# A chunked RWKV attention and token mixer on one Trainium2 core: recurrent state held as diagonal blocks, V of one batch loaded whole, and a new order of steps

## The chip, the cores and the metric

The kernel runs on one core of a Trainium2 chip. The metric is the device time of that core in microseconds, the median of the runs shown. The kernel before takes 106.95 us (three runs, 106.95 to 108.07). Inputs and output are float32 in device memory; the products inside are bf16 with float32 sums.

## The reference

Two layers follow each other. The first is a linear attention with a state of 48 x 48 for each of 4 batches and 8 heads; the second mixes the tokens of a batch:

```python
for t in range(S):                                   # S = 768, heads H = 8, D = 48
    cur = einsum('bhd,bhe->bhde', u * k[t], v[t])
    y[t] = einsum('bhd,bhde->bhe', r[t], state + cur)
    state = w[t][..., None] * state + einsum('bhd,bhe->bhde', k[t], v[t])
x = y.transpose(0, 2, 1, 3).reshape(B, S, H * D)     # 4 x 768 x 384
wq, wk = x @ w_q, x @ w_k                            # 64 wide
mixed = (wq @ wk.T) * scale @ x
out = relu(mixed) @ w_out
```

## The kernel before

**Tiling.** A unit is 256 tokens of one batch (two chunks c = 0, 1 of 128), so there are 12 units, three per batch. Two heads (a pair hp, with hh = 0, 1) share the 128 partitions: head hh lies in partitions 64 hh to 64 hh + 47. Function `unit` adds the steps of one unit to a plan: loads of w, k, r, v (384 KB each); logarithm of w (`f_ln`), cast of k and r (`f_c16`), a triangular product that sums the logarithms (`f_cw`), its exponentials `ep` and `en`; transposes of k and r on TensorE (`f_rawT`), RT = r * ep, KT = k * en, scores A = KT x RT per chunk (`f_A`) and their mask (`f_am`), the state, the output `y`, then X, its transpose, and the q and k of the mixer (`f_qk`). The last unit of a batch also forms T = wk' x X over the six chunks (`f_T`), and from it three blocks of relu, output product and store (`f_mx`, `f_rl`, `f_fp`, `f_os`, `f_st`).

**State.** `f_sn` adds the old state (one product with the identity, 384 columns) and four products of 96 columns, one per head pair. These also give the two blocks that mix the heads of a pair. `f_sb` multiplies by `ptm`, which holds the decay for a head's own columns and zero for the other head's; `ptm` is made on GpSimd (`f_ptm`). So the four products of 96 columns with the old state in `f_y` can take all 128 partitions at once.

**V.** A token pair lies in one partition after the ordinary load (runs of 384 bytes). For V the tokens must be put apart. Units whose digit in `DIRECT` (L339) is 0 (five of them) do so with a cast on GpSimd (`f_v16`), a product with a permutation (`f_vp`) and a copy (`f_vb`). The seven others load V with four DMAs of 96 KB in runs of 192 bytes (`load_v`, L226) and need one cast (L562).

**Order.** Nothing is ordered at run time but by semaphores. Each engine has an in-order queue, and so has SP, which issues the loads and stores. The list `RANK` gives each step its place in its engine's queue, and `ENG` the engine where there is a choice. `Plan.order` walks the queues with assumed durations, to assign PSUM banks and to emit the instructions. Tiles of loads rotate over four buffers, most others over two. `warm` adds products with a zero tile Z: 26 after the first unit's steps and 16 at the end, beside nine before the first step.

**Set-up.** L245 to L293 fill constants and clear padded tiles on DVE, ahead of everything else in its queue; the first useful step there is the cast of k (L475).

Of the kernel before, what the change touches and what calls it, by code (L numbers as in the profile page):

```python
# [14 lines left out]
AX = mybir.AxisListType  # L15
# [9 lines left out]

class Plan:

    def __init__(self, kinds, switch):
        self.kinds = kinds
        self.switch = switch
        self.steps = []

    def add(self, eng, dur, rank, fn, after=(), fill=None, read=(), lag=100, mode=0,
            behind=None):
        s = dict(mode=mode, behind=behind, eng=eng, dur=dur, rank=rank, fn=fn, after=[a for a in after if a is not None],  # L40
                 fill=fill, lag=lag, n=len(self.steps), out=[])
        s["buf"] = None if fill is None else dict(readers=[])
        self.steps.append(s)
        for a in read:
            self.reads(s, a)
        return s

    def dma(self, issue, dur, rank, fn, after=(), fill=None, read=()):

        i = self.add("SP", issue, rank, fn, after, fill, read, lag=0)  # L50
        m = self.add("DQ", dur, 0, self.nothing, [i], lag=0)
        return i, self.add(f"L{m['n']}", 1950, 0, self.nothing, [m], lag=0)

    def nothing(self):
        pass

    def reads(self, s, a, own=False):

        if not own:
            s["after"].append(a)  # L60
        if a["buf"] is not None:
            a["buf"]["readers"].append(s)

    def order(self):
        never = 1 << 60
        queues = {e: [] for e in ("PE", "ACT", "DVE", "POOL", "SP")}
        for s in sorted(self.steps, key=lambda s: s["rank"]):
            if s["eng"] in queues:
                queues[s["eng"]].append(s)
            for a in s["after"]:  # L70
                a["out"].append(s)
        free = dict.fromkeys(queues, 0)
        free["DQ"] = 0
        place = dict.fromkeys(queues, 0)
        rings, owners, moved, done, mode = {}, [None] * 8, [], [], 0

        def clear(buf):

            if buf is None:
                return 0  # L80
            return max([x.get("end", never) for x in buf["readers"]], default=0)

        def start(s):

            if any("end" not in a for a in s["after"]):
                return never, None
            if s["behind"] is not None and "start" not in s["behind"]:
                return never, None
            t = max([free[s["eng"]]] + [a["end"] for a in s["after"]])
            if s["behind"] is not None:  # L90
                t = max(t, s["behind"]["start"])
            if s["eng"] == "SP" and len(moved) >= 3:
                t = max(t, moved[-3])
# [13 lines left out]
            if s["fill"] is not None:  # L107

                ring, size = rings.setdefault(s["fill"], []), self.kinds[s["fill"]]
                if len(ring) >= size:  # L110
                    t = max(t, clear(ring[-size]))
# [7 lines left out]
        while True:  # L119
# [7 lines left out]
            if at is not None:  # L127
                s["buf"]["bank"] = at
                for x in range(at[0], sum(at)):
                    owners[x] = s["buf"]  # L130
            elif s["fill"] is not None:
                rings[s["fill"]].append(s["buf"])
            change = e == "PE" and s["mode"] != mode
            if e == "PE":
                mode = s["mode"]
            run(s, t, s["dur"] + self.switch * change)
            if e == "SP":
                for m in s["out"]:
                    if m["eng"] == "DQ":
                        run(m, max(free["DQ"], s["end"]), m["dur"])  # L140
                        moved.append(free["DQ"])
                        for x in m["out"]:
                            if x["eng"].startswith("L"):
                                run(x, m["end"], x["dur"])
        assert len(done) == len(self.steps)
        return done


@with_exitstack
def kernel(  # L150
# [14 lines left out]
    C = 128  # L165
# [9 lines left out]
    HW = H * D2  # L175

    SHIFT = 25
    MU = -SHIFT * math.log(2.0) / C

    def mm(o, l, rr, start=True, stop=True, trans=False):  # L180
        nc.tensor.matmul(o, l, rr, start=start, stop=stop,  # L181
                         skip_group_check=True, is_transpose=trans)
# [4 lines left out]
    sm = ctx.enter_context(tc.tile_pool(name="sm", bufs=3))  # L187
    bt = ctx.enter_context(tc.tile_pool(name="bt", bufs=2))
# [6 lines left out]
    NB = 4  # L195
    WG = [const([C, HW], F32, f"wg{i}") for i in range(NB)]
    RG = [const([C, HW], F32, f"rg{i}") for i in range(NB)]
    KG = [const([C, HW], F32, f"kg{i}") for i in range(NB)]
    VG = [const([C, HW], F32, f"vg{i}") for i in range(NB)]
    NOS = 4  # L200
    OS = [const([C, 2 * DM], F32, f"os{i}") for i in range(NOS)]
    EW = 132

    KDS = [const([C, 1024], BF16, f"kd{i}") for i in range(2)]
    LW = [const([C, 2 * H * 64], BF16, f"lw{i}") for i in range(2)]
    R16 = [const([C, 2 * H * 64], BF16, f"r16{i}") for i in range(2)]
    K16 = [const([C, 2 * H * 64], BF16, f"k16{i}") for i in range(2)]
    QK = [const([C, NU * 384], BF16, f"qk{i}") for i in range(2)]
    TS = [const([C, DM], BF16, f"ts{i}") for i in range(2)]
    EP = [const([C, 8 * EW], BF16, f"ep{i}") for i in range(2)]  # L210
# [9 lines left out]

    def load_v(b, i, tl):

        for c in range(2):
            src = v[b, :, ds(i * U + c * C, C)].rearrange("h (q j) d -> j q h d", j=2)
            for j in range(2):
                nc.sync.dma_start(out=view(tl, c * DM, [[D, H], [1, D]], p0=64 * j, pn=64),  # L226
                                  in_=src[j])
# [6 lines left out]
    ID16 = const([C, C], BF16, "ID16")  # L234
    Z = const([C, 512], BF16, "Z")
    US = const([C, C], F32, "US")
    CM = const([C, 2 * C], BF16, "CM")
    PM = const([C, 2 * C], BF16, "PM")
    MB = const([C, 2], F32, "MB")
    pos0 = const([C, 1], mybir.dt.int32, "pos0")  # L240
    pos1 = const([C, 1], mybir.dt.int32, "pos1")
    gx = const([C, 1], F32, "gx")
    gv = const([C, 1], F32, "gv")

    nc.vector.memset(Z, 0.0)  # L245
    for _ in range(9):
        mm(PS[:, ds(0, 512)], Z[:, ds(0, C)], Z)
    nc.vector.memset(uT, 0.0)  # L248
    for hh in range(2):
        nc.scalar.dma_start(out=view(uT, hh, [[2, NP], [1, 1]], p0=hh * 64, pn=D),  # L250
                            in_=dataclasses.replace(u, offset=hh * D,
                                                    ap=[[1, D], [D2, NP], [1, 1]]))

    nc.vector.memset(CM, 1.0)
    nc.vector.memset(US, 1.0)
    nc.vector.memset(ID16, 0.0)
    nc.vector.memset(PM, 0.0)
    for t in LW:
        nc.vector.memset(t, 0.0)
    for t in TS:  # L260
        nc.vector.memset(t[64:128, :], 0.0)
    for t in EP:
        nc.vector.memset(view(t, 0, [[EW, 8], [1, 1]]), 1.0)
    for t in R16 + K16 + KDS:
        nc.vector.memset(t, 0.0)  # L265
    nc.vector.memset(MB, 0.0)
    nc.vector.memset(MB[0:D, 0:1], 2.0 ** -SHIFT)
    nc.vector.memset(MB[64:64 + D, 1:2], 2.0 ** -SHIFT)

    for j in range(2):  # L270
        nc.gpsimd.iota(pos0[ds(64 * j, 64), :], pattern=[[0, 1]], base=j, channel_multiplier=2)
        nc.gpsimd.iota(pos1[ds(64 * j, 64), :], pattern=[[0, 1]], base=j + 1,
                       channel_multiplier=2)
    nc.scalar.activation(gx, pos0, ACT.Exp, bias=0.0, scale=MU)
    nc.scalar.activation(gv, pos1, ACT.Exp, bias=0.0, scale=-MU)
    for c in range(2):
        for j in range(2):
            m = view(CM, j * C, [[64, 2], [1, 64]], p0=c * 64, pn=64)
            nc.gpsimd.affine_select(m, m, pattern=[[1, 2], [2, 64]], compare_op=ALU.is_ge,
                                    fill=0.0, base=-j, channel_multiplier=-2)  # L280
    for c in range(2):
        for j in range(2):
            m = PM[ds(c * 64, 64), ds(j * C + j * 64, 64)]
            nc.gpsimd.affine_select(m, m, pattern=[[1, 64]], compare_op=ALU.not_equal,
                                    fill=1.0, base=0, channel_multiplier=-1)
    nc.gpsimd.affine_select(ID16, ID16, pattern=[[1, C]], compare_op=ALU.not_equal, fill=1.0,
                            base=0, channel_multiplier=-1)
    for j in range(2):
        m = view(US, 0, [[64, 2], [1, 64]], p0=j * 64, pn=64)
# [627 lines left out]
```

## Time and profile before

| what | value |
|---|---|
| median of three runs | 106.95 us |
| span of the profiled execution, first to last instruction | 105.2 us |
| granted TensorE clock | 1.000 |
| products with the zero tile Z | 51 |
| ACT waiting for a load of w | 5.1 us in 4 waits |
| GpSimd waiting for loads of v, k and r | 4.5 + 2.0 + 1.5 us, and 1.4 us for v in the seven units of `load_v` |
| last ordinary load issued | about 72 us (r), V of the last unit 77 to 80 us |
| DMA issues of V: 384 KB / 96 KB | 5 / 28 |

The span is measured inside the execution. The 1.75 us between it and the median lie before the first and after the last instruction. PE is TensorE, DVE the vector engine, ACT the scalar engine, POOL GpSimd; SPq is SP's queue. All TensorE instructions have line L181 since one helper issues them, so they are told apart by their operands.

### The profile page before, as it was taken

Reading aid. Unit: us, or ns where it says so; the run is one execution under the profiler, and the core shown is the slowest. Engines: PE = TensorE matmul, PEld = TensorE weight load, DVE = VectorE, ACT = ScalarE, POOL = GpSimd, SP = SyncE. Lnnn points to the kernel's source line nnn. Section 1 sums busy time; section 2 is a strip of 40 time slices with the busy share of each in tenths; the row PEclk is TensorE's granted clock in tenths of the full one; section 3 lists DMA queues with packets and bytes.
Section 4 is the critical chain, followed back from the end, with each engine's and each line's share of the span. In section 5 each row is a group of like instructions: output and inputs, shape, how many; then the busy total and the mean of one; then the engine's idle time right before and its main releaser. Section 6 shows DMA issues by size and latency. Waiting matters only on the chain.

```text
span 105.2 us, 3714 instructions
## 1 busy us (share of the span) xinstructions
PE 96.2 (91%) x1506; PEld 70.2 (67%) x1506; DVE 88.1 (84%) x138; ACT 79.9 (76%) x123; POOL 71.0 (67%) x92
## 2 busy tenths in 40 slices
PE   5969889997999998999997897779999999998995
PEld 2246566686887786968796775658697987856551
DVE  6898997898999999798999996786998889754740
ACT  4367778797989868997899959867898895954610
POOL 6600859599997996979979993968689699000000
DMA  1999999999999898989997969998997870033564
GB/s 28 298 324 325 325 323 270 238 297 175 312 316 264 148 272 230 288 172 310 325 311 142 213 123 269 350 289 209 288 255 143 303 307 18 0 153 150 199 243 160
DMA packets 61217, 24.62 MB, mean 234 GB/s; under 512 B 58896, under 2 KB 60048, under 8 KB 61200
## 3 DMA queue, kind: packets, MB, share of 16 engines
q1 hardware_dynamic: 60640, 24.19, 85.5%
q10 hardware_dynamic: 560, 0.20, 0.7%
q8 instruction: 11, 0.18, 0.7%
q14 instruction: 6, 0.05, 0.1%
HBM read 19.66 MB, written 4.72 MB: 232 GB/s over the span
## 4 chain that ended last, share of the span: by engine, by line
PE 51%; DVE 14%; DMA 13%; issue 7%; POOL 5%; ACT 4%; SPq 4%; DVEq 0%; ACTq 0%; POOLq 0%
PE PS L181 51%; DMA wg<-in_w_dram 7%; DMA kg<-in_k_dram 6%; SPq L226 3%; DVE SB L666 2%; DVE RT L536 2%; POOL KT L547 2%; DVE qT L529 2%; DVE KT L547 2%; POOL Vd L601 1%; ACT MX L381 1%; SPq L230 1%; ACT kd L373 1%; DVE X L707 1%; DVE kd L265 1%
## 5 line engine op out<-in xcount | busy, mean ns | idle before, releaser
L619 DVE TENSOR_TENSOR AM<-PS,US 128x1024 bf16<-128x1024 f32 x24 | 28.9, 1220 | 1.1 <-PE PS L181 0.7
L547 POOL TENSOR_TENSOR KT<-ks,en 128x1024 bf16<-128x1024 bf16 (+1 forms) x10 | 19.3, 1934 | 1.2 <-ACT en L498 0.6
L601 POOL TENSOR_TENSOR Vd<-VB,dd 128x768 bf16<-128x768 bf16 (+1 forms) x14 | 18.4, 1318 | 2.2 <-ACT dd L371 1.3
L181 PE MATMUL PS<-Z 128*128 128x512 bf16 x51 | 16.2, 424 | 1.5 <-DVE uT L248 1.2
L707 DVE SCALAR_TENSOR_TENSOR X<-PS,gx,Vd 128x768 bf16<-128x768 f32 (+1 forms) x13 | 12.3, 955 | 3.3 <-PE PS L181 2.8
L181 PEld LDWEIGHTS <-KT 48*128 48x128 bf16 (+1 forms) x272 | 10.7, 95 | 6.3 <-issue 3.8
L467 ACT ACTIVATE lw<-wg 128x768 bf16<-128x768 f32 x12 | 10.0, 846 | 5.5 <-DMA wg<-in_w_dram 5.1
L181 PE MATMUL PS<-wo,MX 128*128 128x384 bf16 x72 | 13.5, 326 | 0.1
L504 ACT ACTIVATE ep<-PS 128x1024 bf16<-128x1024 f32 (+1 forms) x14 | 12.7, 922 | 0.9 <-PE PS L181 0.9
L498 ACT ACTIVATE en<-PS 128x1024 bf16<-128x1024 f32 (+1 forms) x14 | 12.5, 904 | 0.5 <-issue 0.3
L666 DVE TENSOR_TENSOR SB<-PS,ptm 128x384 bf16<-128x384 f32 x20 | 11.1, 553 | 1.5 <-PE PS L181 1.3
L181 PE MATMUL PS<-RT,KT 48*128 48x128 bf16 x192 | 9.2, 217 | 1.4 <-POOL KT L547 0.5
L381 ACT ACTIVATE MX<-PS 128x768 bf16<-128x768 f32 (+1 forms) x12 | 8.7, 730 | 1.8 <-PE PS L181 1.7
L475 POOL CAST r<-rg 128x768 bf16<-128x768 f32 x10 | 8.7, 870 | 1.6 <-DMA rg<-in_r_dram 1.5
L475 POOL CAST k<-kg 128x768 bf16<-128x768 f32 x9 | 7.4, 825 | 3.3 <-DMA kg<-in_k_dram 2.0
L181 PE MATMUL PS<-ID,k 128*128 128x128 bf16 x96 | 7.4, 220 | 2.2 <-POOL k L475 1.4
L181 PEld LDWEIGHTS <-MX 128*128 128x128 bf16 x72 | 6.7, 98 | 3.9 <-issue 0.3
L373 ACT ACTIVATE kd<-PS,gv 128x384 bf16<-128x384 bf16 (+1 forms) x11 | 8.1, 740 | 1.4 <-PE PS L181 1.3
L181 PEld LDWEIGHTS <-Z 128*128 128x128 bf16 x51 | 5.0, 105 | 6.0 <-issue 2.3
L371 ACT COPY os<-PS 128x768 f32<-128x768 f32 (+1 forms) x10 | 7.1, 708 | 2.5 <-PE PS L181 2.2
L536 DVE TENSOR_TENSOR RT<-PS,ep 128x1024 bf16<-128x1024 bf16 (+1 forms) x14 | 8.4, 609 | 0.5 <-PE PS L181 0.2
L181 PE MATMUL PS<-CM,lw 64*128 64x128 bf16 x192 | 7.8, 223 | 1.1 <-ACT XT L371 0.7
(82 smaller groups left out, 211.4 us busy)
## 6 DMA issues: line engine op xcount, KB each, us to landing
wg<-in_w_dram SPq DMA_DIRECT2D x12, 384.0 KB, 5.3
kg<-in_k_dram SPq DMA_DIRECT2D x12, 384.0 KB, 5.0
rg<-in_r_dram SPq DMA_DIRECT2D x12, 384.0 KB, 5.1
out_dram<-os SPq DMA_DIRECT2D x9, 384.0 KB, 4.3
vg<-in_v_dram SPq DMA_DIRECT2D x28, 96.0 KB, 3.7
vg<-in_v_dram SPq DMA_DIRECT2D x5, 384.0 KB, 5.0
out_dram<-os SPq DMA_DIRECT2D x5, 192.0 KB, 2.0
wof<-in_moe_w_out_dram SPq DMA_DIRECT2D x1, 576.0 KB, 5.7
```

Source lines behind the costliest of these rows:

```text
L181: nc.tensor.matmul(o, l, rr, start=start, stop=stop, skip_group_check=True, is_transpose=trans)
L381: nc.scalar.activation(o, i, ACT.Relu)
L467: nc.scalar.activation(view(lw, 0, [[64, H], [512, 2], [1, D]]), view(wg, 0, [[D2, H], [D, 2], [1, D]]), ACT.Ln, bias=0.0, scale=math.exp( ...
L475: op(view(dst, 0, [[64, H], [512, 2], [1, D]]), view(src, 0, [[D2, H], [D, 2], [1, D]]))
L498: nc.scalar.activation(sb("en", [C, 1024])[:, cols(cs, 512)], t["cw"][:, cols(cs, 512)], ACT.Exp, bias=0.0, scale=-1.0)
L504: nc.scalar.activation(view(ep, cs[0] * NP * EW + 66, [[EW, NP * len(cs)], [-65, 2], [1, 64]]), t["cw"][:, cols(cs, 512)], ACT.Exp, bias=0 ...
L536: nc.vector.tensor_tensor(view(sb("RT", [C, 1024]), cs[0] * 512, [[C, n4], [64, 2], [1, 64]]), view(t["rT"], cs[0] * 512, [[C, n4], [64, 2 ...
L547: e.tensor_tensor(sb("KT", [C, 1024])[:, cols(cs, 512)], t["ks"][:, cols(cs, 512)], t["en"][:, cols(cs, 512)], ALU.mult)
L601: nc.gpsimd.tensor_tensor(sb("Vd", [C, 2 * DM])[:, cols(cs, DM)], t["VB"][:, cols(cs, DM)], view(t["dd"], cs[0] * H, [[1, len(cs) * H], [0 ...
L619: nc.vector.tensor_tensor(view(sb(f"AM{c}", [C, 1024]), 0, [[C, 8], [1, C]]), view(t[f"A{c}"], 0, [[C, 8], [1, C]]), view(US, 0, [[0, 8], ...
L666: nc.vector.tensor_tensor(view(x, 0, [[D, H], [1, D]]), view(t[f"sn{c}"], 0, [[D, H], [1, D]]), view(t["ptm"], c * 8, [[1, 8], [0, D]]), A ...
L707: nc.vector.scalar_tensor_tensor(view(X["t"], (2 * i + c0) * DM, [[DM, ncs], [1, DM]]), view(t["y"], c0 * 512, [[512, ncs], [1, DM]]), gx, ...
```

## The change

The step planner and `unit` are written anew; the arithmetic that is kept has the same instructions. What differs:

- **State.** The state tile has 192 columns: head hh of pair hp in partitions 64 hh on, columns 48 hp on. `kd` is stored with zeros around each head, so that a window of 128 columns puts a head's result into the right partitions; eight products of 48 columns take the place of four of 96. The decay is read from `ep`; `ptm` and its constant are gone. The factor that was in `ptm` moves into `kd` and the identity.
- **Output.** The state's part of y becomes products over 48 partitions (`yi`), four for each chunk and head half, issued ahead of the scores' part (`ya`). A second half that goes to the same chunk is preceded by a drain of TensorE. 
- **T.** The two chunks of a unit go to two halves of the array's columns and of the output partitions.
- **V.** `DIRECT` is gone. Nine units use the ordinary load, permutation and copy. The last batch's V (three units) is loaded by four DMAs of 288 KB in runs of 192 bytes, in two steps of the plan.
- **Set-up.** Only the padding is cleared, and only part of it before the second tiles' turn; the permutation's constant is made later on POOL.
- **Fillers.** 12 products with Z, all ranked within the first two units' steps; none at the end. The nine before the first step stay.
- **Order.** New `RANK` and `ALT` (engine choices), planned with 1190 ns for a load in the first three units and 1440 after, where 1440 stood for all (1780 for the first).

The instructions' order on PE has 92 changes between whole-array products and those on part of it (cw, vp, A, yi, T), against 56 in the trace of before. SP issues, after the loads of units 0 to 3: `vw` (V of the last batch) behind k of unit 11, then the first store, then w and r of unit 11.

```diff
-    mm(x[:, ds(0, DM)], ID16, old.tile, start=True, stop=False)
-    for hp in range(NP):
-        mm(x[:, ds(hp * D2, D2)], KDS[n % 2][:, ds((c * NP + hp) * C, C)],
-           t["VB"][:, ds(c * DM + hp * D2, D2)], ...)
+    mm(x[:, ds(0, NP * D)], IDU, old.tile, start=True, stop=False)
+    for hp in range(NP):
+        for hh in range(2):
+            h = 2 * hp + hh
+            mm(x[:, ds(hp * D, D)],
+               kd.tile[:, ds(64 + (c * H + h) * 128 - 64 * hh, 128)],
+               VB.tile[:, ds(c * DM + h * D, D)],
+               start=(old is None and h == 0), stop=(hh == 1))
...
-    nc.vector.tensor_tensor(view(x, 0, [[D, H], [1, D]]), view(t[f"sn{c}"], 0, [[D, H], [1, D]]),
-                            view(t["ptm"], c * 8, [[1, 8], [0, D]]), ALU.mult)
+    nc.vector.tensor_tensor(view(SB.tile, 0, [[D, NP], [1, D]]), view(at(sn), 0, [[D, NP], [1, D]]),
+                            view(ep.tile, c * NP * EW + 64, [[EW, NP], [0, D]]), ALU.mult)
...
-    for hp in range(NP):
-        mm(y[:, ds(c * 512 + hp * D2, D2)], t["RT"][:, ds((c * NP + hp) * C, C)],
-           old.tile[:, ds(hp * D2, D2)], start=False, stop=True)
+    sides = [[(0, 0), (1, 1)], [(1, 0), (0, 1)]]
+    def f_yi(e, side=side, cs=cs, first=not yis[cs[0]]):
+        if not first:
+            nc.tensor.drain()
+        for hp in range(NP):
+            for c, hh in side:
+                mm(of(c, 2 * hp + hh), RT.tile[ds(hh * 64, D), ds((c * NP + hp) * C, C)],
+                   olds[c].tile[ds(hh * 64, D), ds(hp * D, D)], ...)
...
-    mm(batch["T"][:, ds(0, DM)], batch["QK"][:, ds(ii * 384 + c * DH, C)], ...)
+    mm(at(T)[ds(c * DH, DH), ds(0, DM)], QK.tile[:, ds(ii * QS + U + c * DH, DH)], ...)
...
+    def load_whole(b, q, tl):
+        n_ = H // 2 * NCH
+        for j in range(2):
+            nc.sync.dma_start(
+                out=view(tl, q * n_ * D, [[D, n_], [1, D]], p0=64 * j, pn=64),
+                in_=dataclasses.replace(v, offset=(b * H * S + j) * D + q * n_ * C * D,
+                                        ap=[[D2, 64], [C * D, n_], [1, D]]))
...
+    for x in (tiles["lw"][0], tiles["k16"][0], tiles["r16"][0]):
+        nc.vector.memset(view(x, D, pads), 0.0)
+    for x in tiles["ep"]:
+        nc.vector.memset(view(x, 0, [[EW, 8], [1, 1]]), 1.0)
+    nc.vector.memset(US, 1.0)
...
+    for x in (tiles["lw"][1], tiles["k16"][1], tiles["r16"][1]):
+        nc.vector.memset(view(x, D, pads), 0.0)
+    nc.vector.tensor_scalar_mul(IDU, ID16, UNIT)
...
+    for x in tiles["kd"]:
+        nc.vector.memset(x[:, ds(0, 64)], 0.0)
+        nc.vector.memset(view(x, 64 + D, [[128, 16], [1, 128 - D]]), 0.0)
...
+    for x in range(WARM):
+        z = bank()
+        s_ = add(("z", x), {"E": 216}, lambda e, z=z: mm(at(z), Z[:, ds(0, C)], Z), [], z, [], lag=0)
```

## The prediction

> **What bounds the kernel now.** I read the engines' totals first, then the stages, then the chain of waits, then the order of time on single engines.
>
> ```profile
> PE 96.2 (91%) x1506; PEld 70.2 (67%) x1506; DVE 88.1 (84%) x138; ACT 79.9 (76%) x123; POOL 71.0 (67%) x92
> DMA  1999999999999898989997969998997870033564
> GB/s 28 298 324 325 325 323 270 238 297 175 312 316 264 148 272 230 288 172 310 325 311 142 213 123 269 350 289 209 288 255 143 303 307 18 0 153 150 199 243 160
> DMA packets 61217, 24.62 MB, mean 234 GB/s; under 512 B 58896, under 2 KB 60048, under 8 KB 61200
> ```
>
> TensorE looks most loaded, DVE follows closely. The DMA engines read "busy" until 84 us, but what they move drops from 325 to 123-175 GB/s once for nearly every V that is loaded apart. The stages say when this hurts:
>
> ```profile
> 56.00:64.00 8.00, 6.35 (x121) 4.99 (x122) 7.72 (x12) 6.74 (x11) 6.88 (x7) 1.00 0.78 162
> 64.00:72.00 8.00, 6.55 (x112) 5.07 (x112) 6.16 (x8) 6.44 (x9) 6.20 (x6) 1.00 1.06 303
> 72.00:80.00 8.00, 8.00 (x145) 6.59 (x144) 7.21 (x10) 6.97 (x11) 6.35 (x9) 1.00 0.99 246
> ```
>
> The first number after the stage's length is PE. From 56 to 72 us PE loses 3.1 us; from 72 on it is full (to 93 us in the chain). The chain of waits names the loss:
>
> ```profile
> 58.41 0.63 SPq L226
> ...
> 59.09 1.58 SPq L226
> ...
> 60.72 0.72 SPq L226
> ...
> 63.30 6.31 DMA kg<-in_k_dram
> ...
> 69.66 0.84 POOL k L475
> ```
>
> SP is held by issues of L226, so k of a later unit starts late, and PE waits for its cast. Elsewhere PE runs back to back, so its own work counts. I took that from starts in order of time, since a busy time includes the latency of a product:
>
> ```profile
> 18.18 0.40 PE L181 MATMUL PS<-RT,KT 48*128 48x128 bf16 x8
> 18.41 0.49 PE L181 MATMUL PS<-v,PM 64*128 64x384 bf16 x4
> 18.83 0.35 PE L181 MATMUL PS<-UB,qT 128*128 128x2 bf16 x8
> 20.99 0.40 PE L181 MATMUL PS<-RT,KT 48*128 48x128 bf16 x8
> 21.32 0.62 PE L181 MATMUL PS<-ID,k 128*128 128x128 bf16 x8
> ```
>
> Eight scores take 0.23 us when another partial-array group follows, and 0.33 us when whole-array transposes follow: leaving part of the array costs 0.10 us. Over the trace, 24 entries and 27 exits without an idle each stretch a group by 0.10 us at the median. In such starts a kd group of four (96 columns) takes 0.17, an RT group with the old state 0.17, the identity (384 columns) 0.16, eight AM products (48 columns) 0.20, six T products 0.97, a permutation 0.33. All groups at their shortest sum to 74.1 us; 56 changes of mode add 5.6: **79.7 us** (the page has 80.0 without Z). PE's first group starts at 5.30, its last ends near 100.7. So 105.2 = 5.3 + 79.7 + 15.7 of gaps and fillers + 4.5 of last copy, store and end. The 15.7 are: 5.2 before 16 us (11 fillers among them, groups done there sum to 5.5), 3.4 of 16 later fillers at 0.215, 3.1 from 56 to 72, and 4.0 of small waits.
>
> **What the Trainium skill says.** TensorEngine Tiling, Key Properties: a change of tiling mode drains TensorE; the 0.10 us above agrees. The same page, Restrictions and Gotchas: row tiles cannot access one PSUM bank at the same time, hence the drain before `yi`'s second half; no run here shows its price. TensorE: Matmul & The Clock Gate, the section on the 56 ns gap: starts are never under about 25 ns apart, however narrow the product; 0.20 us for eight AM products agrees. DMA: Bandwidth & Descriptors, Specifications: line rate needs 512 bytes or more; the trace agrees in direction, 325 GB/s with 384-byte runs, about 150 with 192.
>
> **The change part by part, PE.**
> - Out: 20 RT groups x 0.17 = 3.4; 20 kd groups x 0.17 = 3.4; 16 identities x 0.16 = 2.6; 24 T products at 0.163 = 3.9. Sum 13.3.
> - State in: 160 products x 26 ns (as AM) = 4.1; 16 identities of half width 0.083 = 1.3. Sum 5.4.
> - `yi` in: 160 products. The scores' groups run two row halves side by side (0.23/8 = 29 ns for 128 columns, against 55 for a whole-array transpose), so I take half of AM's 26 ns, 2.1 us. Bounds: 2.1, and 4.2 if starts keep 26 ns. Twelve or so drains: none is in the trace; 0 at least, 0.18 us each at most (an AM product's whole latency is 183 ns), I take 0.10, 1.2 us.
> - T: column halves are not in the trace; 2.0 if two run together, 3.9 if not. I take 2.0.
> - V: four units more with a permutation, 1.3.
> - Mode changes: the new queue has 92, against 56: 36 x 0.10 = 3.6.
>
> In: 5.4 + 2.1 + 1.2 + 2.0 + 1.3 + 3.6 = 15.6, so PE **gains work, +2.3 us** (bounds -1 where drains and some changes fall into waits, +7.3 at the upper prices). It lies on the path wherever PE is full.
>
> **DVE.** The state's multiply: 553 ns at 384 columns and 1220 for AM's 1024 make 1.04 ns per column, so 353 ns at 192: 20 x 0.20 = -4.0. By the new engine letters: kd -3 more on DVE (+1.8), ks +0.7, QK +1.1, T's copy +1.1, relu +0.55, KT -1.1, output copies -2.05, XT and dd -0.7: +1.4. After set-up DVE has 2.6 less than its 82.0. That pays nothing while PE is full, but PE's small waits are mostly for DVE and ACT; I give 0.7 of the 4.0.
>
> **Set-up.** DVE's first cast starts at 7.16. Padding alone: three pairs of tiles from 485 ns down to some 170 (bounds 165 and 272, the rows of 128 words and of 256 bf16), kd 0.7 (1.35 if not in words) in place of 485, T's tiles and MB gone. The queue ends near 6.0 (5.3 to 7.3); k lands near 5.6 (w at 4.4 plus one load of 1.2). I take 1.0 us earlier. The permutation's 4 x 236 ns move behind on POOL, which waited until 10.6 for V anyway.
>
> **Other engines.** POOL loses 14 `ptm` (3.1), gains two k casts (1.65), one r cast less (-0.9), about 1.1 of KT: -1.3, from 71. ACT gains four V copies (3.2) and two output copies (1.75), loses casts of k, kd and ks: within 1 of 79.9. Neither becomes the bound.
>
> **DMA and SP.** 384 bytes x 16 engines / 325 GB/s = 18.9 ns per packet and engine; the same pace with 192 bytes gives 162 GB/s, as the dips show. So packets count: before 41 x 1024 + 7 x 2048 = 56,320; after 45 x 1024 + 6,144 = 52,224. 4096 / 16 x 18.9 = -4.8 us of transfer. SP issues 5 + 28 V loads before, 9 + 4 after. Whole V stands behind k of unit 11: at an unbroken pace it lands at 4.4 + 42 x 1.21 + 2.4 (weights) + 7.3 = 65 us; its first reader on POOL had its V at 72.5 before, so 7 us are left for buffer waits. If it were late, k, r and Vd behind it on POOL would wait. The first store stands ahead of w of unit 11; it held SP there before as well. I give 2.1 of the 3.1 us from 56 to 72, since SP still waits for buffers.
>
> **Fillers.** The 15 behind the last product (100.7 to 104.1) end with the store: 0. Of the 16 later ones (3.4 us) I give 2.2, as some covered waits that stay. In the first units 12 replace 11: 0.
>
> **Sum.** Gaps 15.7 - 1.0 - 2.2 - 2.1 - 0.7 = 9.7. Span 5.3 + (79.7 + 2.3) + 9.7 + 4.5 = 101.5. The median is 1.75 above the profiled span, so **103.3**.
>
> **The rivals.**
> - *It packs better.* Drains and mode changes fall into waits and the freed DVE shortens more gaps: PE 81, gaps 7.5, span 98.3, **100.1**. For it: DVE and DMA both get lighter. Against: PE was idle only 1.1 us from 24 to 56 us.
> - *Given back.* PE takes 5 us more at middling prices, gaps shrink by 5: **107**. For it: PE is full from 70 to 93 us, where four units' `yi` fall.
> - *Slower: TensorE becomes the bound.* `yi` at 26 ns, T without overlap, drains at 0.18: 79.7 + 7.3 = 87.0; the order laid out for cheaper steps then misses its places, and gaps come only to 12. Span 5.3 + 87.0 + 12 + 4.5 = 108.8, **110.5**. It decides from the point where PE's added work passes what the gaps give back (some 6 us, plus the 1% margin). Against it: the scores show that row halves overlap.
> - *Loads aren't relieved.* Whole V holds SP and the DMA engines for 7 us in one piece just when w and r of unit 11 are due. Then the 2.1 us stay: **105.4**; within the range.
>
> **How the numbers follow.** Likeliest case 103.3 (with 105.4 as its late-load end; own range 101 to 105.5): chance 0.47. Better packing 0.20, given back 0.16, slower 0.17. A measurement of this kernel tells about 1% from no change, 105.9 to 108.0. Faster by over 1%: 0.47 + 0.20 + 0.01 of the third = 0.68; within: 0.14; slower: 0.18. The range leaves out the far half of the best case and of the slow one: 99.0 to 108.8.
>
> **What would show it.** Right: PE's groups plus changes near 82 us and full from 16 us on; no SP issue of V in the chain; `SB` near 353 ns; first cast on DVE near 6.0; packets near 57,100; the last load landed before 78 us. Wrong: `yi` groups of eight over 0.15 us, or drains over 0.15 us; T still 0.97 us; POOL waiting long for whole V; new waits of PE for ACT in the middle; PE's gaps above 12 us.

## The result and the profile after

The changed kernel takes **106.16 us** (median of 13 runs, 105.28 to 107.58) beside 107.83 for the kernel before measured beside it (13 runs): ratio **0.986** [0.982, 0.990]. Two repeats gave 0.988 [0.984, 0.991] and 0.989 [0.983, 0.996]. So it is faster, as forecast, but by 1.4% and not by 3.4%. A ratio takes of each kernel only the runs within 1.5% of its fastest (2 of 6 of e12_state_undone below, 3 of 6 of e14_no_perm, 6 of 27 of before in the batch of e15 to e17, whose three ratios therefore stand about 1% high), a median takes all. Before's median moved between 107.7 and 108.6 from batch to batch, so kernels are compared by ratio or within a batch.

The first view is the page of the profiled execution (span 104.4, time 106.1 us): totals, the slices of the granted clock, the DMA engines.

```profile
PE 93.2 (89%) x1651; PEld 69.4 (66%) x1652; DVE 84.4 (81%) x140; ACT 80.6 (77%) x122; POOL 69.3 (66%) x80
PEclk9999999999589999999999999999999999999999
DMA  1999999999999988999999799999993056004791
DMA packets 56803, 24.65 MB, mean 236 GB/s; under 512 B 54480, under 2 KB 55632, under 8 KB 56784
```

Every engine but ACT has less to do, packets fell to 56,803 (forecast 57,100). But the clock falls to half in the eleventh slice and the first part of the twelfth, which the trace of before doesn't show; in the later batches 150 runs of before had a mean clock of 0.983 to 1.000. The stages, first of before, then of after (busy time of PE, PEld, DVE, ACT, POOL, then clock, DMA share, GB/s):

```profile
16.00:24.00 8.00, 7.74 (x136) 5.51 (x134) 6.99 (x10) 7.08 (x10) 6.75 (x9) 1.00 1.02 266
24.00:32.00 8.00, 7.31 (x150) 6.23 (x149) 7.41 (x10) 7.11 (x11) 7.55 (x8) 1.00 1.10 272
```

```profile
16.00:24.00 8.00, 5.79 (x134) 4.55 (x131) 6.97 (x11) 5.90 (x8) 6.42 (x6) 1.00 1.05 278
24.00:32.00 8.00, 7.57 (x129) 5.80 (x128) 5.78 (x8) 6.85 (x10) 8.00 (x8) 0.79 1.07 295
56.00:64.00 8.00, 7.54 (x155) 5.98 (x156) 7.00 (x11) 6.34 (x13) 5.96 (x6) 1.00 0.96 249
64.00:72.00 8.00, 7.74 (x159) 6.31 (x156) 7.72 (x12) 7.44 (x10) 8.00 (x8) 1.00 0.99 202
72.00:80.00 8.00, 7.79 (x189) 6.85 (x186) 7.56 (x11) 6.93 (x12) 5.98 (x6) 1.00 0.98 282
```

From 56 to 72 us PE was short by 3.1 us and is short by 0.7: that part came as forecast. From 16 to 24 us PE lost 2 us of busy time (fillers that are gone), yet it has no more products done. The chain of waits says why:

```profile
15.83 1.05 ACT ep L491
16.88 0.62 SPq L292
...
17.55 5.83 DMA vg<-in_v_dram
...
23.53 0.83 POOL v L556
...
24.41 1.89 PE PS L240 x40
...
88.06 11.64 PE PS L240 x122
```

SP issues V of unit 2 only at 17 us, it lands at 23.4, and PE stands before the permutation of V of unit 2 (vp.2). No SP issue of V stands in the chain after that. PE in order of time shows the wait and the halved clock behind it (start, latency, operands; the bracket is the idle time before):

```profile
13.76 0.61 PE L240 MATMUL PS<-ID,KT 128*128 128x128 bf16 x8
14.21 0.61 PE L240 MATMUL PS<-ID,r 128*128 128x128 bf16 x8
...
22.44 0.37 PE L240 MATMUL PS<-VB,AM 128*128 128x48 bf16 x8
24.41 0.50 PE L240 MATMUL PS<-v,PM 64*128 64x384 bf16 x4 [1.59 <-POOL v L556]
24.84 0.40 PE L240 MATMUL PS<-ID,KT 128*128 128x128 bf16 x4
...
26.79 1.03 PE L240 MATMUL PS<-ID,KT 128*128 128x128 bf16 x8
27.75 0.61 PE L240 MATMUL PS<-RT,KT 48*128 48x128 bf16 x8
```

The eight products with KT and the identity at 26.79 (transposes of KT, from which `kd` is made) need 0.96 us until the next group starts; the same eight at 13.76 need 0.45.

**Where the time went, by PE's own account.** For each stage I take elapsed time, less each group at its shortest, less 0.10 us per change of mode, as the prediction did; fillers count as gap. Both kernels are worked in the same way; before's tail comes out 0.3 longer than in the prediction's sum.

| us | before | forecast | after |
|---|---|---|---|
| first PE group | 5.3 | 5.3 | 5.9 |
| PE work (groups + changes) | 79.4 | 82.0 | 81.7 |
| gaps and fillers, 5 to 16 us | 4.3 | | 3.2 |
| 16 to 40 | 4.7 | | 6.1 |
| 40 to 56 | 1.4 | | 0.3 |
| 56 to 72 | 3.7 | | 1.5 |
| 72 to the last group | 1.7 | | 0.8 |
| gaps, sum | 15.8 | 9.7 | 11.8 |
| tail | 4.8 | 4.5 | 4.9 |
| span | 105.2 | 101.5 | 104.4 |

The miss of 2.9 us of span is gaps +2.1, first group +0.6, tail +0.4, PE work -0.3. By stage, the forecast's terms leave 3.3 us of gaps up to 16 us, 2.5 from 16 to 40, 1.6 from 56 to 72 and 2.4 in the rest. So the stage from 16 to 40 us misses by 3.6, and the rest, with 1.1, gives 1.3 more than was forecast. Of the 6.1 us some 1.7 are the halved clock (0.79 over 8 us).

### The profile page after: what moved, and what is told of

Its sections match the earlier page's. It is cut to its first block, busy times and chain, and to the rows that moved or that the text cites. A ratio compares the mean times of both kernels' runs of the same rounds, so it can differ in the third digit from the quotient of the medians.

```text
span 104.4 us, 3964 instructions
## 1 busy us (share of the span) xinstructions
PE 93.2 (89%) x1651; PEld 69.4 (66%) x1652; DVE 84.4 (81%) x140; ACT 80.6 (77%) x122; POOL 69.3 (66%) x80
## 2 busy tenths in 40 slices
DMA packets 56803, 24.65 MB, mean 236 GB/s; under 512 B 54480, under 2 KB 55632, under 8 KB 56784
## 4 chain that ended last, share of the span: by engine, by line
PE 74%; DMA 6%; POOL 5%; DVE 5%; issue 3%; ACT 2%; SPq 1%; POOLq 0%; DVEq 0%
PE PS L240 74%; DMA vg<-in_v_dram 6%; DVE KT L539 2%; POOL KT L539 2%; POOL v L556 2%; POOL Vd L588 1%; ACT ep L491 1%; ACT MX L396 1%; DVE RT L531 1%; DVE AM L608 1%; SPq L292 1%; DVE qT L522 1%; ACT os L384 0%; DVE Z L306 0%; POOL r L463 0%
## 5 line engine op out<-in xcount | busy, mean ns | idle before, releaser
L539 POOL TENSOR_TENSOR KT<-ks,en 128x1024 bf16<-128x1024 bf16 (+1 forms) x11 | 20.5, 1864 | 3.6 <-DVE ks L390 3.4
L463 POOL CAST k<-kg 128x768 bf16<-128x768 f32 x11 | 9.0, 825 | 3.3 <-DMA kg<-in_k_dram 3.3
L384 ACT COPY os<-PS 128x768 f32<-128x768 f32 (+1 forms) x13 | 8.6, 680 | 2.5 <-PE PS L240 2.2
L463 POOL CAST r<-rg 128x768 bf16<-128x768 f32 x9 | 7.5, 835 | 4.3 <-DMA rg<-in_r_dram 2.3
L556 POOL CAST v<-vg 128x768 bf16<-128x768 f32 x9 | 7.4, 825 | 3.6 <-DMA vg<-in_v_dram 3.6
L522 DVE TENSOR_TENSOR qT<-PS,ks 128x1024 bf16<-128x1024 bf16 x12 | 8.2, 681 | 0.4 <-issue 0.4
L240 PE MATMUL PS<-Z 128*128 128x512 bf16 x20 | 7.4, 511 | 1.2 <-DVE uT L309 1.2
L384 ACT COPY XT<-PS 128x768 bf16<-128x768 bf16 (+1 forms) x9 | 6.9, 765 | 2.0 <-PE PS L240 2.0
L240 PE MATMUL PS<-ID,r 128*128 128x128 bf16 x96 | 7.7, 226 | 0.4 <-POOL r L463 0.3
L240 PE MATMUL PS<-VB,AM 128*128 128x48 bf16 x192 | 7.9, 184 | 0.1
```

Source lines behind the costliest of these rows:

```text
L240: return nc.tensor.matmul(o, l, rr, start=start, stop=stop, skip_group_check=True, is_transpose=trans)
L384: nc.scalar.copy(o, i)
L463: op(view(o.tile, 0, [[64, H], [512, 2], [1, D]]), view(g[src].tile, 0, [[D2, H], [D, 2], [1, D]]))
L539: x.tensor_tensor(KT.tile[:, cols], ks.tile[:, cols], en.tile[:, cols], ALU.mult)
L556: v16s = add(("v16", n), {"P": 826}, lambda e: nc.gpsimd.tensor_copy(view(v16.tile, 0, [[D, H], [DM, 2], [1, D]]), view(g["vg"].tile, 0, [ ...
```

## The experiments

Unless said otherwise, each is the changed kernel with the edit named; the ratio is to the kernel before.

| kernel | median us (runs) | ratio | before in that batch |
|---|---|---|---|
| e1_fill6 | 105.81 (6) | 0.988 [0.980, 0.995] | 107.67 |
| e2_v2first | 107.01 (22) | 0.998 [0.994, 1.002] | 107.67 |
| e3_nofill | 106.22 (6) | 0.989 [0.980, 0.998] | 107.67 |
| e5_before_nofill | 107.14 (22) | 1.004 [1.000, 1.008] | 107.67 |
| e6_no_v23 | 104.69 (6) | 0.969 [0.962, 0.976] | 108.61 |
| e9_before_v_one | 104.08 (6) | 0.963 [0.956, 0.970] | 108.61 |
| e10_pe12 | 107.43 (20) | 0.994 [0.990, 0.997] | 108.61 |
| e11_half_loads | 104.98 (6) | 0.973 [0.965, 0.981] | 108.61 |
| after_again (unchanged) | 106.48 (22) | 0.988 [0.984, 0.991] | 108.00 |
| e12_state_undone | 105.09 (6) | 0.969 [0.964, 0.975] | 108.00 |
| e13_start_fill6 | 106.29 (22) | 0.986 [0.982, 0.990] | 108.00 |
| e14_no_perm | 105.78 (6) | 0.981 [0.971, 0.990] | 108.00 |
| e15_yi_beside | 106.84 (22) | 0.999 [0.994, 1.004] | 108.29 |
| e16_state_masked | 104.85 (6) | 0.977 [0.965, 0.988] | 108.29 |
| e17_no_state_no_perm | 105.65 (6) | 0.987 [0.978, 0.997] | 108.29 |
| after_third (unchanged) | 106.00 (6) | 0.989 [0.983, 0.996] | 108.04 |
| e16_again | 105.29 (6) | 0.982 [0.972, 0.992] | 108.04 |
| e18_masked_fill6 | 104.70 (6) | 0.979 [0.972, 0.986] | 108.04 |

**Is it the wait for V of unit 2?** First theory: the 1.59 us wait and the halved clock behind it cost the missing 1.5 us. Six fillers ahead of vp.2 keep PE busy through the wait; another kernel issues that V before w of unit 4.

```diff
-WARM = 12
+ZRANK = [1, 2, 4, 5, 7, 8, 10, 11, 12, 13, 21, 22, 46.5, 46.51, 46.52, 46.53, 46.54, 46.55]
+WARM = 18
```

> The changed kernel with six more products with the zero tile (1.3 us at 0.216 each) on TensorE just ahead of the permutation of V of unit 2, where TensorE sits idle for 1.59 us in the trace of the changed kernel. Theory A (the stall at 22.8 us lets the granted clock fall to half for 3.4 us, which costs 1.7 us that nothing gives back): granted clock 1.000, ratio to the kernel before down from 0.986 to about 0.972 (1.5 us less). Theory B (TensorE's loss there is made good by later waits, the order as a whole sets the time): clock 1.000, but the ratio stays within 0.983 to 0.989.

```diff
+    moves = {('vg', 2): 13.5}
+    for s_ in plan.steps:
+        s_["rank"] = moves.get(s_["key"], s_["rank"])
```

> The changed kernel with one swap in SP's order: V of unit 2 is loaded ahead of w of unit 4. Theory A: V lands one load (about 1.3 us) earlier, most of the 1.59 us stall goes and the clock stays at 1.000, ratio about 0.965 (2 to 2.5 us less than the changed kernel). Theory B: the wait moves to w of unit 4 on the scalar engine (1.14 us there already) and TensorE loses the same time one group later, ratio 0.983 to 0.989, whether or not the clock falls.

The six fillers did hold the clock (0.986 to 1.000 over the runs, beside 0.959 to 0.993), but the ratio stayed at 0.988. With V of unit 2 first, the wait went over to w of unit 4, the gap from 24 to 32 us grew from 1.9 to 4.3, and the kernel lost 1%. The theory fell: here the move of one load only changed which load was waited for. (The six fillers alone are worth 0.35 us at most by the medians, 105.81 beside 106.16 in another batch.)

**Do the fillers cost or give anything?** One kernel without the 12 fillers of the changed order; one is the kernel before without its 42.

```diff
-WARM = 12
+WARM = 0
```

> The changed kernel without its 12 fillers, so that only the nine products before the first step remain. Theory A (fillers hold the clock): the clock falls to half also among the first groups, between 6 and 16 us, mean clock 0.95 or lower, and the time rises by 1 to 3 us (ratio 1.00 to 1.01). Rival (fillers cost what they take): the first group starts 0.6 us earlier, at 5.3 us, the rest is as before, ratio 0.980 to 0.986.

```diff
+    for s in plan.steps:
+        if s["fn"].__qualname__.split(".")[-2:] == ["<locals>", "f"] and "warm" in s["fn"].__qualname__:
+            s["fn"], s["dur"], s["fill"], s["buf"] = plan.nothing, 0, None, None
```

> The kernel before without its 26 + 16 fillers, the nine at the start kept. The step of the prediction under test gave 2.2 us of gain to the 16 later fillers. If that step is right, this kernel is faster, ratio 0.980 to 0.985. If the fillers hold the clock (theory A), the granted clock falls below 1.000 and the time is the same or longer, ratio 1.00 to 1.03.

Neither moved the time clear of noise: before without its fillers has ratio 1.004, and a median 0.5 us below before's. Its clock fell below 1.000 in all 22 runs (0.947 to 0.999), so a rival is that the fillers' time was gained and lost again to the clock. The runs speak against it: the 11 with the higher clock (0.975 or more) have a median of 107.12 us, the other 11 one of 107.15. The stage of the kernel before, without fillers:

```profile
16.00:24.00 8.00, 6.84 (x134) 5.49 (x132) 7.38 (x11) 7.68 (x11) 7.01 (x9) 0.96 1.00 263
24.00:32.00 8.00, 6.50 (x133) 5.44 (x134) 6.76 (x9) 6.39 (x10) 6.93 (x8) 1.00 1.06 251
```

PE is busy 1.7 us less in these 16 us, and the gap by the account above, 16 to 40 us, is 4.6 as with them (4.7). Where the group of scores near 24.5 us waits for KT, it starts at nearly the same time with and without fillers, first before, then e5_before_nofill:

```profile
24.78 0.40 PE L181 MATMUL PS<-RT,KT 48*128 48x128 bf16 x8 [0.54 <-POOL KT L547]
```

```profile
24.41 0.40 PE L181 MATMUL PS<-RT,KT 48*128 48x128 bf16 x8 [0.64 <-POOL KT L547]
```

The 16 fillers (15 of them stand between 16 and 41 us) had stood in waits that stay. This is the term of the forecast that failed.

**What do the loads bound?** Three kernels cut or join loads. The first has the six fillers and no V for units 2 and 3 (their products read zeros). The second is the kernel before with each of the seven V loads that it splits in four as one load of 384-byte runs, so its rows of V are in another order. The third has the six fillers, and every ordinary load from unit 4 on brings half of the heads.

```diff
-    lambda e, ap=ap, x=g[name].tile: load(b, i, x, ap),
+    lambda e, ap=ap, x=g[name].tile, skip=(name == "vg" and n in (2, 3)):
+    None if skip else load(b, i, x, ap),
```

> The changed kernel with six fillers ahead of the permutation of V of unit 2 (as e1_fill6, so that the clock stays at 1.000), and with the loads of V of units 2 and 3 left out: their tiles are set to zero on GpSimd at the start, so the output lacks those two units' values. All later loads move up by 2 x 1.2 us. Theory C (from 16 to 40 us TensorE waits for loads, which is why neither the fillers nor the held clock moved the time by more than 0.4 us): TensorE's gaps between 16 and 40 us fall from 4.9 to 3 us or less, ratio to the kernel before about 0.97 (e1_fill6: 0.988). Theory D (these gaps are waits of the engines for one another, with the loads hidden): gaps stay at 4.5 to 5, ratio 0.984 to 0.990.

```diff
-    lambda tile_=tile_: load_v(b, i, tile_), fill=name)
+    lambda tile_=tile_, ap=ap: load(b, i, tile_, ap), fill=name)
```

> The kernel before, its seven V loads of four 96 KB DMAs each replaced by one DMA of 384-byte runs; the token pairs of those units then stay in one partition, so V of these units is left in the wrong order. Everything else is the same. The prediction's step on DMA and SP: 7 x 1024 packets and 21 issues fewer; TensorE's gaps from 56 to 72 us fall from 3.7 to about 1.5 us, packets near 54,050, and the ratio is 0.97 to 0.98. Rival (the loads' lateness is hidden by other waits): gaps from 56 to 72 us move elsewhere, ratio 0.99 to 1.00.

```diff
-    lambda e, ap=ap, x=g[name].tile: load(b, i, x, ap),
+    lambda e, ap=ap, x=g[name].tile: load(b, i, x, ap, 8 if n < 4 else 4),
```

> e1_fill6 with the loads of w, k, r and v halved from unit 4 on (four of eight heads; the other four keep an earlier unit's values, so the output lacks those heads; V of the last batch is loaded in full). Theory C extended (loads hold the kernel over its whole length): the time falls by 2 us or more, ratio 0.965 or lower. Rival (after 40 us TensorE's own work is the bound): the gaps up to 40 us shrink a little, the time falls by less than 1 us, ratio 0.979 to 0.988.

Two early loads less are worth 1.8% by the ratios (0.969 beside 0.988) and 1.1 us by the medians, in different batches. The gaps from 16 to 40 us fell by about 0.8 us only, not to 3 us as expected if loads held this stage. So the loads count there, but that they are the whole of it isn't shown. Half of all later bytes is worth 1.5% at most (0.973, between the two expectations). With one load for each of the seven V, the kernel **before** is 4 us faster, 0.963. Its stages:

```profile
56.00:64.00 8.00, 7.11 (x146) 5.59 (x141) 7.65 (x12) 7.63 (x12) 7.83 (x10) 1.00 1.02 268
64.00:72.00 8.00, 8.00 (x145) 6.56 (x144) 7.69 (x10) 7.29 (x11) 7.10 (x7) 1.00 1.09 307
```

PE is short by 0.9 us where it was short by 3.1, and the gap from 56 to 72 us goes from 3.7 to 0.8. That is more than the whole change gives, but it isn't the change's own V part. It takes 7,504 packets out (61,217 to 53,713) and asks for no permutation; the change takes 4,414 out and pays for four more permutations with their copies. By packets alone the 4 us would be 2.4 us for the change, an estimate from these two counts. No run has the change's V part by itself. Whether another part takes something back is asked next.

**Is it PE's added work?** First its price: 12 products with Z (2.6 us) spread over 35 to 93 us, on top of the six fillers.

```diff
-WARM = 12
+ZRANK = F6 + [90.5 + 10 * i for i in range(12)]   # F6: the 18 ranks of e1_fill6
+WARM = 30
```

> e1_fill6 with 12 more products with the zero tile, one after every tenth step of TensorE's queue from about 35 to 93 us: 12 x 0.216 = 2.6 us of work for TensorE alone. If TensorE is the bound from 32 us on (the prediction's ground for putting PE's added 2.3 us on the path): the time rises by 2 to 2.6 us, ratio 1.007 to 1.012. If it has slack (waits take the work in): a rise under 1 us, ratio 0.988 to 0.996.

The ratio rose by 0.6% over e1_fill6, the medians by 1.6 us, in different batches: added PE work comes out at a quarter to six tenths of its length, so PE has slack there. Then the state's form and the permutation were taken out, each alone, beside the changed kernel as it is and a kernel whose fillers z.0 and z.1 stand behind PE's first group, cw.0 (the sums of logarithms of unit 0). Without the permutation the tile VB also has four buffers in place of two.

> The changed kernel as it is, beside the next three on one chip, so that they can be read against it. Every theory: a ratio to the kernel before near 0.986, 0.98 to 0.99.

```diff
-                for hp in range(NP):
-                    for hh in range(2):
-                        h = 2 * hp + hh
-                        mm(x[:, ds(hp * D, D)], kd.tile[:, ds(64 + (c * H + h) * 128 - 64 * hh, 128)], ...)
+                for hp in range(NP):
+                    mm(x[:, ds(hp * D2, D2)], kd.tile[:, ds((c * NP + hp) * C, C)],
+                       VB.tile[:, ds(c * DM + hp * D2, D2)], ...)
...
-                if not first:
-                    nc.tensor.drain()
-                for hp in range(NP):
-                    for c, hh in side:
-                        mm(of(c, 2 * hp + hh), RT.tile[ds(hh * 64, D), ds((c * NP + hp) * C, C)], ...)
+                for c in cs if first else ():
+                    for hp in range(NP):
+                        mm(of(c, 2 * hp, 2), RT.tile[:, ds((c * NP + hp) * C, C)],
+                           olds[c].tile[:, ds(hp * D2, D2)], ...)
```

> The changed kernel with the state back in 384 columns: four whole-array products of 96 columns and a copy product of 384 for sn, VectorE's SB over 384 columns, four whole-array products for yi, no drain and no mode change for yi. The mask that kept the two heads of a pair apart is left out, and with it the off-diagonal blocks are not zero. Theory C (the state's new form takes back what the loads give, by PE's mode changes): PE work falls by about 2 us (some 40 mode changes x 0.10 go, sn and yi get dearer by 2), and the ratio falls to 0.97. Theory D (the state's form gains, since VectorE does 4 us less and PE's cost is even): the ratio rises above that of the changed kernel by 1 to 3%. Theory E (the permutation of V takes it back): the state is worth under 1% either way.

```diff
-ZRANK = [1, 2, 4, 5, ...]
+ZRANK = [3.1, 3.2, 4, 5, ...]
```

> The changed kernel with fillers z.0 and z.1 put behind cw.0, and six more fillers ahead of vp.2. Start theory: the first PE group starts at 5.3 us of the span, as forecast, not at 5.91, and the span is shorter by about 0.6 us than that of the kernel with the six fillers alone (103.4); ratio near 0.98. Rival: the first cast of k on VectorE, near 6.1, is the bound behind it, and the time stays as it is; ratio 0.986.

```diff
-        RT=(2, 1024, BF16), KT=(2, 1024, BF16), v16=(2, 2 * DM, BF16), VB=(2, 2 * DM, BF16),
+        RT=(2, 1024, BF16), KT=(2, 1024, BF16), v16=(2, 2 * DM, BF16), VB=(4, 2 * DM, BF16),
...
-                view(v16.tile, 0, [[D, H], [DM, 2], [1, D]]),
+                view(VB.tile, 0, [[D, H], [DM, 2], [1, D]]),
...
             def f_vp(e):
+                return
...
-            VBs = add(("VB", n), copies(2 * DM), lambda e: copy(...), [vps], VB, [vp])
+            VBs = add(("VB", n), copies(2 * DM), lambda e: None, [vps], VB, [vp])
```

> The changed kernel with the permutation of V left out in units 0 to 8: GpSimd's cast writes the tile that the products read, the nine vp groups and the nine VB copies go, and V keeps the row order of its load, so the sums over rows pair other rows. Theory E (the permutation takes back what the loads give): PE loses nine groups of 0.34 us and their mode changes, about 4 to 5 us of work, ScalarE and VectorE 7 us, and the time falls by 3 to 4 us, ratio 0.95 to 0.96. Theory C: PE loses the same work, but only its share on the path counts, 1 to 2 us, ratio 0.97 to 0.975.

With z.0 and z.1 moved the first PE group does start at 5.23, but the time stays. The cast of k on DVE starts at 6.03 and isn't what holds the second group: four fillers now stand ahead of it, and it starts at 7.57, where it started at 6.91 in the changed kernel. So this run doesn't test what an earlier start is worth. The kernel without fillers (e3_nofill) says more: its first groups start earlier and then wait for casts and for ACT's logarithm of w, so that the second group of logarithm sums starts at 9.01, beside 9.19 in the changed kernel. First e13_start_fill6, then e3_nofill:

```profile
6.20 1.53 PE L241 MATMUL PS<-Z 128*128 128x512 bf16 x4
7.57 0.61 PE L241 MATMUL PS<-ID,k 128*128 128x128 bf16 x8
```

```profile
6.48 0.62 PE L241 MATMUL PS<-ID,k 128*128 128x128 bf16 x8 [0.57 <-DVE k L464]
7.53 0.62 PE L241 MATMUL PS<-ID,r 128*128 128x128 bf16 x8 [0.43 <-DVE r L464]
9.01 1.04 PE L241 MATMUL PS<-CM,lw 64*128 64x128 bf16 x16 [0.86 <-ACT lw L454]
```

Without the permutation PE has about 3.6 us less to do (nine groups of 0.33 and six changes of mode), and the median is 0.7 us lower (105.78 beside 106.48). The intervals overlap, so that a gain isn't shown, and both expectations, 0.95 to 0.96 and 0.97 to 0.975, were missed. Its profiled execution took 107.96 us, 2.2 above its median, so its gaps don't explain this.

The state in its old form has a median **1.4 us** lower (105.09 beside 106.48), and the intervals lie apart, though VectorE has 2 us more to do (86.3 us busy beside 84.4):

```profile
PE 90.9 (88%) x1491; PEld 67.3 (65%) x1492; DVE 86.3 (83%) x138; ACT 80.5 (78%) x122; POOL 69.4 (67%) x80
```

**What of the state's new form costs?** Ten groups moved so that yi stands next to other row-tiled groups; the state put back with its mask on GpSimd; both parts out.

```diff
+    MOVES = {('kT', 4): ('A', 3, 0), ('yi', 1, 1, 0): ('ya', 1, 1), ('yi', 3, 1, 0): ('qk', 2),
+             ('A', 5, 0): ('yi', 4, 0, 0), ('yi', 5, 1, 0): ('ya', 5, 0), ('yi', 6, 1, 0): ('qk', 4),
+             ('cw', 9): ('yi', 7, 0, 0), ('A', 9, 1): ('yi', 8, 0, 0), ('dps', 9): ('yi', 8, 1, 0),
+             ('yi', 10, 1, 0): ('T', 8, 0)}
+    rank_of = {s_["key"]: s_["rank"] for s_ in plan.steps}
+    for s_ in plan.steps:
+        if s_["key"] in MOVES:
+            s_["rank"] = rank_of[MOVES[s_["key"]]] + 0.5
```

> The changed kernel with ten PE groups moved by a few places, so that the yi groups stand next to other row-tiled groups (A, cw, vp) or after T: some 18 of the 92 mode changes go, and the drains between neighbouring halves are covered by the group between them. Theory C (TensorE's time for mode changes counts on the path): PE work falls by about 1.8 us and the time by 0.5 to 1.5 us, ratio 0.974 to 0.982. Rival (only the products' and VectorE's waits count): within 0.3% of the changed kernel, ratio 0.985 to 0.99.

```diff
+                nc.gpsimd.tensor_tensor(
+                    view(ptm[n % 2], cs[0] * 8, [[2, n4], [1, 2]]),
+                    view(ep.tile, cs[0] * NP * EW + 64, [[EW, n4], [0, 2]]),
+                    view(MB, 0, [[0, n4], [1, 2]]), ALU.mult)
```

> The changed kernel with the state in 384 columns, now with the mask of the kernel before (a small GpSimd operation for each KT, 14 of about 0.2 us), so that it computes the whole. Theory C: as in the kernel without the mask, ratio near 0.97, at most 0.5% above it. Rival (the mask left out is what gained there): ratio 0.98 to 0.99, as the changed kernel.

The third joins the diffs of e12_state_undone and e14_no_perm.

> The changed kernel with both left out: the state in 384 columns without its mask, and V without its permutation in units 0 to 8. If the two costs add (1.8% and 0.7%), the ratio is near 0.962, which is that of the kernel before with V in whole loads (0.9626). If they lie beside one another, so that only one of them counts, it stays at 0.969 or above. If the permutation was hidden only by TensorE's load, it is below 0.955.

Thirteen mode changes fewer (79) took 1.7 us out of PE's work, and the gaps grew by 1.6: no gain. Since the moves also make other groups wait, this doesn't free the mode changes of blame; it shows that to take them away at this price gives nothing. The masked state gains 2.0 us on e15_yi_beside in its batch, so the missing mask was not the gain. With the permutation out as well, nothing is gained beyond the state (105.65 beside 104.85). One more batch for the size, with the six fillers added in a third kernel:

> The changed kernel as it is, a third time, so that the next two can be read against it on the same chip: 106 to 106.6 us.

> The changed kernel with the masked state in 384 columns, again. If the state's new form costs 1.3 us, as two kernels of six runs each say, the median is near 105 us and at least 1% below the changed kernel's of this batch. Rival (the two sets of six were lucky): within 0.5% of it.

> The changed kernel with the masked state in 384 columns and six fillers ahead of vp.2, which covers TensorE's wait for V of unit 2. If the halved clock behind that wait costs 1 us in the runs that have it, the median falls below the masked kernel's by 0.3 to 0.6 us and stays above 0.985 of full clock in all runs; rival: the fillers change nothing (within 0.3 us), as in the kernel before without its fillers.

Here the masked state gains 0.7 us, between the two expectations (at least 1%, or within 0.5%), and with the fillers 1.3. The fillers' share of 0.6 is what was expected if the halved clock costs, but the two sets of six overlap. So the old form was faster in all three batches: than the changed kernel by 1.4 and 0.7 us, than e15_yi_beside by 2.0. The intervals lie apart in the first two and overlap in the last; about 1 us is what I take from it. The old form's runs often have the higher clock, but that isn't likely to be the reason: with the clock held by fillers in both forms (0.986 or more in every run) the ratios are 0.979 (e18_masked_fill6) and 0.988 (e1_fill6), in different batches, with intervals that overlap. e18_masked_fill6, with whole V, the permutation, T in halves and the state's old form, leaves nothing of the computation out and is the fastest such kernel here: 104.70 beside 106.00 and 108.04. Its page:

```profile
PE 92.5 (90%) x1498; PEld 67.4 (66%) x1498; DVE 86.0 (84%) x141; ACT 80.2 (78%) x122; POOL 72.5 (71%) x94
PEclk9999999999999999999999999999999999999999
```

## Why the prediction was right in direction and wrong in size

- **The step that failed** is "Fillers": "Of the 16 later ones (3.4 us) I give 2.2, as some covered waits that stay". Those 2.2 us are worth nothing that the runs show: the kernel before without any filler runs at 1.004 [1.000, 1.008], with a median 0.5 us lower. In the changed kernel the stage where most of them stood, 16 to 40 us, has 6.1 us of gaps against 4.7, where the forecast needed some 2.5. They had covered waits, and the sum counted a cover as a cost. The 2.2 us are the greater part of the 3.6 missed in that stage. The other 1.4 came new with the changed order, and its wait for V of unit 2 with the halved clock behind it stands there. Six fillers in that wait gave no clear gain.
- **Luck.** The gaps from 40 to 56 us and from 72 us on fell by 2.0 us, where 0.7 was forecast for DVE. No run says what gave the other 1.3; without it the miss would have been larger.
- **First group**: the span was summed with 5.3, measured is 5.9, as z.0 and z.1 stand ahead of cw.0 now. What these 0.6 us cost isn't shown: in e3_nofill, which starts at 5.19, the lead is down to 0.18 us by the second group of logarithm sums.
- **PE work +2.3**: measured +2.3 (79.4 to 81.7). T's six products take 0.61 us, two halves at once, where they took 0.97, and `yi`'s groups of eight 0.12, as forecast. So two row halves side by side start every 15 ns, and the floor of about 25 ns, which the prediction took from the Trainium skill (TensorE: Matmul & The Clock Gate, the section on the 56 ns gap) and kept as an upper bound, doesn't hold for them. Where both halves of `yi` stand together the drain shows:

```profile
48.31 0.62 PE L240 MATMUL PS<-SB,RT 48*128 48x48 bf16 x16
48.86 0.57 PE L240 MATMUL PS<-VB,AM 128*128 128x48 bf16 x16
...
49.98 0.28 PE L240 MATMUL PS<-SB,RT 48*128 48x48 bf16 x8
50.19 0.62 PE L240 MATMUL PS<-ID,k 128*128 128x128 bf16 x8
...
86.48 0.68 PE L240 MATMUL PS<-X,QK 128*64 128x384 bf16 x6
87.09 0.28 PE L240 MATMUL PS<-SB,RT 48*128 48x48 bf16 x8
87.21 0.39 PE L240 MATMUL PS<-RT,KT 48*128 48x128 bf16 x8
```

  Eight need 0.12 before another group on part of the array and 0.21 before a whole-array group, with the 0.10 of leaving. Sixteen need 0.55, so the drain is about 0.55 - 0.22 - 0.10 = 0.23 us. That is above the 0.18 given as its most, but only where nothing stands between the halves. That row tiles need it, as the Trainium skill says (TensorEngine Tiling, Restrictions and Gotchas), no run here puts to the test.
- **56 to 72 us, -2.1**: measured -2.2, so the size held. That the loads of V had caused these gaps is shown on the kernel before, where one load for each V takes 2.9 us out of them.
- **DVE**: SB is 0.352 us (forecast 0.353), first cast at 6.11 (forecast near 6.0, less than 7.16), gaps before 16 us -1.1 (forecast -1.0):

```profile
4.94 0.59 DVE L347 MEMSET kd<- 128x640 uint32 x1
6.11 0.56 DVE L463 CAST k<-kg 128x768 bf16<-128x768 f32 x1 [0.58 <-DMA kg<-in_k_dram]
```

  The cast now waits for k. The state's form spares DVE 4 us in SB; what these are worth by themselves isn't shown, but with the old form, and SB at its old cost, the kernel is faster.
- **Rivals.** "Given back" had the right shape, part of the gain going into PE's work, at 106 and not 107; it named `yi`, and the state's form with its `yi` is indeed what costs about 1 us. "Slower" did not come: `yi` ran at 15 ns a product, not 26. "Loads aren't relieved" did not decide: V of the last batch held SP from 63.5 to 71.0 us, later than the 65 us at which the prediction had it landed, and GpSimd then waited 1.93 us for r of unit 11 (79.5 us), but the gaps from 72 us on fell all the same.
- **What is open.** The estimate of 2.4 us for the change's loads less about 1 us for the state's form comes near the 1.7 us measured (107.83 to 106.16), but this is no proof: the estimate scales a run on the kernel before, e17_no_state_no_perm shows that such parts don't simply add, and the set-up, T and the new order weren't taken out one by one. Which part of the state's form costs, its 18 mode changes, its drains or its 160 more products, wasn't separated: e15_yi_beside moved other work along with them.

## What to carry to other kernels

Before a filler, or any product without use, is counted as gained time, take it out of the old kernel and look: where it stands in a wait that stays, it costs nothing. Price a change's parts one at a time: here the state's form spared DVE 4 us and yet cost about 1 us, hidden in a change that was faster as a whole. Where several loads are due close together, an earlier issue of one can make another late, as with V of unit 2 here; fewer bytes or packets did give time.

## What the hardware showed besides

- After the 1.59 us wait PE's clock fell to half: 0.79 as a mean over 24 to 32 us is 3.4 us at half. The Trainium skill (TensorE: Matmul & The Clock Gate, What's actually happening) has the clock fall after an idle window of about 3.4 us; PE here was never idle for that long at a stretch. Groups took twice as long, yet a price for it doesn't stand out. Six fillers that kept the clock up gave 0.988 beside 0.986, and among 22 runs of the unchanged kernel the fastest (104.99 us) had a mean clock of 0.973 and one with 0.983 took 106.17. Against this, the three of e10_pe12's 20 runs with the lowest clock (0.968 to 0.983) were its longest, 109.5 to 110.5 us; which of the two caused the other no run says.
- The 2.6 us of added products cost 0.6 to 1.6 us, and 3.6 us of PE work left out with the permutation gave no more than 0.7 by the medians: on a PE that is 89% busy, work is not time one for one.
